# Four rooms for an expert's w2, fetched a whole expert ahead, in an attention, MoE and soft-MoE kernel

## The chip, the cores and the metric

The kernel runs on one core of a Trainium2 chip. The metric is the device time of one launch in microseconds (us). The profile speaks of the core's engines: PE is TensorE's matmul and PEld its weight load (two activities of one engine), DVE is VectorE, ACT ScalarE, POOL GpSimd and SP SyncE, which issues most of the DMAs of this kernel. "SPq" is SyncE's own queue of DMA issues. A DMA issue waits on SyncE until the room that it writes to is free, and all that is issued after it on SyncE waits behind it.

## What is computed

Three layers, one after the other (cut to what matters here):

```python
# 1. attention: batch 4, heads 8, seq 768, head_dim 64; a local window of +-15 keys
#    and the 24 block maxima of k; its output is x, 3072 x 512
x = attn_out.transpose(0, 2, 1, 3).reshape(3072, 512)

# 2. MoE, N 3072 tokens, D 512, E 8 experts, F 1024, cap N // E = 384 tokens each
logits = x @ w_gate
for idx in np.argsort(-logits.flatten()):        # greedy, best pair first
    tok, e = idx // E, idx % E
    if assigned[tok] < 0 and counts[e] < cap:
        assigned[tok] = e; counts[e] += 1
for e in range(E):
    mask = assigned == e
    out[mask] = np.maximum(x[mask] @ w1[e], 0) @ w2[e]

# 3. soft MoE over 32 slots (8 groups of 4)
logits = out @ phi
d = softmax of logits over tokens;  c = softmax of logits over slots
slot_input = d.T @ out                           # 32 x 512
for e in range(8):
    slot_out[e] = np.maximum(slot_input[e] @ w1s[e], 0) @ w2s[e]
result = c @ slot_out
```

The kernel never forms `out`. For expert e it makes h = relu(x w1), the logits as h (w2 phi), the softmax sums from these, and then (d.T h) w2, which has 32 rows instead of 384. The product of w2 and phi is made ahead of the experts.

## The kernel before, in words

The program has four parts: attention; the routing of tokens (the search, many small steps on VectorE with small matmuls called `as`, of which the later ones are spread over the first experts); the experts; and the tail, which is the slot MLPs and the output. Beside the end of attention and the routing, w2 of all experts is loaded, transposed and multiplied by phi (the matmuls of line 1050 with the copies `wt` of line 1065, and `pp` of line 1015). The w2 tiles of experts 1 to 7 for this lie in the pool `pre`, in rooms with the tag "mw", of which there are NPRE1.

**The experts** run in stages r = 0 to 7 of eight steps (fc 0 to 7). A step multiplies the expert's 384 gathered tokens by 128 columns of w1 (`mm1`, line 1260: twelve matmuls into `ph`, since w1 and x are each split into a high and a low part), and transposes an earlier step's result (`turn_h`, line 1281). w1 comes in 256 KB pieces, `raw`, which lie in four rooms; ScalarE casts each into `wh` (line 1225) and GpSimd or VectorE makes `wl` (line 1227), two steps ahead of their use. SyncE issues `raw` four steps ahead of its cast (line 1211).

**The dispatch of expert r-1** is a generator that runs inside stage r. Each step takes it to its next `yield`, so that the two experts' work stands interleaved on TensorE. Near its end, `aT` (the 32 slots' weights times h, summed) is multiplied by w2: eight matmuls of line 1439 into `pS`, in two halves of four. The first half uses quarters 0 and 1 of w2, the second quarters 2 and 3. A quarter is 512 KB. Quarters lie in rooms with the tag "w2", of which there are two, and so the second half is fetched when the first half's matmuls have been issued in the program (`weights2(r, (2, 3))`), and two yields stand between the halves. The first half of the next expert's w2 is fetched after the second (`weights2(r + 1, (0, 1))`). The trace calls these tiles `w`. For the last expert the second half goes into rooms of `raw`.

**The slot MLPs' weights** are 64 pieces of 512 KB, `mw`. Pieces are loaded beside the experts into rooms that are free by then, NPRE of them first (NPRE0 in one pool, NPRE1 in `pre`, the others in a third pool), paced over the 56 steps of stages 0 to 6, then NLATE more once the search is over; then into rooms that the experts no longer need (those of gathered tokens, wh and wl, x, w2, raw). The tail multiplies piece after piece, and a room that has been read takes a further piece.

What sets the order: from the experts on all five engines run in the order of the program text (`manual_schedule`), so the place of a `yield` or of a `weights2` in a generator is the order on each engine's queue. Before that, ScalarE's order is set by the scheduler.

Of the kernel before, what the change touches and what calls it, by code (L numbers as in the profile page):

```python
# [10 lines left out]
F32 = mybir.dt.float32  # L11
# [11 lines left out]
N, DM, E, F = B * S, H * D, 8, 1024  # L23
CAP = N // E
NT = S // 64
NSLOT = 32
NPRE = 28
NHURRY = 2
NSPLIT = 4
NPRE0 = 8  # L30
LAG = 4
WAIT0 = 600
NPRE1 = 19
NLATE = 5
NRAW = 4
NWHL = 3
# [880 lines left out]
def tile_kernel(  # L917
# [13 lines left out]
    nc = tc.nc  # L931
# [180 lines left out]
    ring = ctx.enter_context(tc.tile_pool(name="ring", bufs=2))  # L1112
# [7 lines left out]
    def slot(pool, tag, bufs=None):  # L1120
        return lambda name, dt=F32: [pool.tile([128, 1024], dt, name=name, tag=tag, bufs=bufs)]
# [3 lines left out]
    def halves(pool, tags, bufs):  # L1125
        HALVES.append(
            lambda name: [
                pool.tile([128, 512], F32, name=f"{name}_{i}", tag=tag, bufs=bufs) for i, tag in enumerate(tags)
            ]
        )  # L1130
        return HALVES[-1]
# [30 lines left out]
    with ExitStack() as c2:  # L1162
        wp = c2.enter_context(tc.tile_pool(name="wp", bufs=2))

        XG, EI, ER, W, W2, PR, RAW = {}, {}, {}, {}, {}, {}, []
# [71 lines left out]
        def weights2(r, qs):  # L1237

            for q in qs:
                src = w2[bass.ds(number(r), 1), 256 * q : 256 * q + 256, :].rearrange("o (t p) d->p (o t) d", p=128)  # L1240
                if r + 1 == E and q > 1:

                    ts = [ring.tile([128, DM], F32, name=f"w2_{r}_{q}{i}", tag="raw", bufs=NRAW) for i in range(2)]
                    for i, t in enumerate(ts):
                        nc.sync.dma_start(t, src[:, i])
                    W2[r, q] = ts
                else:
                    t = ring.tile([128, 2, DM], F32, name=f"w2_{r}_{q}", tag="w2", bufs=2)
                    nc.sync.dma_start(t, src)
                    W2[r, q] = [t[:, 0], t[:, 1]]  # L1250

        HT, H, L4 = {}, {}, {}

# [88 lines left out]
        def dispatch(r):  # L1342
# [92 lines left out]
            for cols in (slice(0, 512),):  # L1435
                pS = ps.tile([128, DM], F32, name=f"pS{r}_{cols.start}", tag="b", bufs=2)
                for fc in range(8):
                    g = fc % 4
                    nc.tensor.matmul(  # L1439
                        pS[32 * g : 32 * g + 32, cols],  # L1440
                        aT[:, fc % 2, 32 * (fc // 2) : 32 * (fc // 2) + 32],
                        W2[r, fc // 2][fc % 2][:, cols],
                        start=fc < 4,
                        stop=fc >= 4,
                    )
                    tick(234)
                    if fc == 3 and not last:
                        weights2(r, (2, 3))
                        yield
                        yield  # L1450
                if last:
                    filler(r, 4)
                    for cols in (slice(0, 256), slice(256, 512)):
                        nc.vector.scalar_tensor_tensor(
                            acc[:, cols], acc[:, cols], al, pS[:, cols], ALU.mult, ALU.add
                        )
            if not last:
                weights2(r + 1, (0, 1))
                if r:
                    nc.vector.scalar_tensor_tensor(den, den, al, ds, ALU.mult, ALU.add)  # L1460
                    nc.vector.scalar_tensor_tensor(acc, acc, al, pS, ALU.mult, ALU.add)
                else:
                    nc.vector.tensor_copy(den, ds)
                    nc.vector.tensor_copy(acc, pS)
# [12 lines left out]
        with tc.manual_schedule(engines=engines):  # L1477
            for _ in work:
                if 0 in PLACED:
                    break  # L1480
            while 0 not in PLACED:
                advance()
            gather(0)
            fetch(NRAW - 1)
            while not PP.get("end"):
                next(work)
            split(1)
            weights2(0, (0, 1))
            for dc in range(4):
                transpose_x(0, dc)  # L1490
                if dc:
                    low_x()
                if dc == 0:
                    next(work, None)
            low_x()
        with tc.manual_schedule(engines=engines | {mybir.EngineType.Activation}):
            for r in range(E):
                search_state["stage"] = r
                if r:
                    fetch_p(r)  # L1500
                fill = dispatch(r - 1) if r else iter(())
                next(fill, None)
                for fc in range(8):
                    split(8 * r + fc + NWHL - 1)
                    fetch(8 * r + fc + NWHL - 1 + NRAW)
                    if r == 0 and fc == 1:
                        fetch_p(r)
                    ahead = fc == 7 and r + 1 in XG
                    if ahead:
                        mm1(r, 7, (lambda: None, lambda: transpose_x(r + 1, 0), lambda: transpose_x(r + 1, 1), low_x))  # L1510
                    elif fc == 4:
                        mm1(r, 4, (lambda: None, lambda: logits(r, 0)))
                    elif r == E - 1 and fc in (2, 3):
                        mm1(r, fc, (lambda: None, lambda: next(fill)))
                    else:
                        mm1(r, fc)
                    if r == E - 1 and fc == 7:
                        logits(r, 1, range(3))
                    if fc == 2:
                        next(fill, None)  # L1520
                    while turned < 8 * r + fc - (2 if 8 * r + fc < 8 * E - 3 else 1) + 1:
                        turn_h(*divmod(turned, 8))
                        turned += 1
                    if ahead:
                        low_x()
                    if fc >= 3 and r + 1 in PLACED and r + 1 not in XG:
                        gather(r + 1)
                    if r == E - 1 and fc == 5:
                        weights2(r, (2, 3))
                    if fc != 2:  # L1530
                        next(fill, None)
                    while early and NPRE - len(early) < (NPRE * (8 * r + fc)) // 56:
                        load_pieces(early.pop(0))
                    if search_state["done"] and not late:
                        right.close()
                        late.append(right.enter_context(tc.tile_pool(name="late", bufs=NLATE, side="right")))
                        later += NLATE * [slot(late[0], "mw")]
                    if later and fc % 2:
                        load_pieces(later.pop())
                    if r == E - 1 and fc == 1:  # L1540
                        load_pieces(part(xp.tile([128, 1536], F32, name="xg_mw", tag="xg"), 0))
                    if r == E - 1 and fc >= 6:
                        load_pieces(halves(ring, ("wh", "wl"), NWHL))
                for _ in fill:
                    pass
                if r + 1 < E:
                    while r + 1 not in PLACED:
                        advance()
                    if r + 1 not in XG:
                        gather(r + 1)  # L1550
                        until = search_state["pe"] + 5000
                        while search_state["ready"] < until:
                            advance()
                        search_state["pe"] = max(search_state["pe"], until)
                    for dc in range(4):
                        if dc > 1 or not ahead:
                            transpose_x(r + 1, dc)
                            if len(LOW) > 1:
                                low_x()
                    while LOW:  # L1560
                        low_x()
                    logits(r, 1)
                else:
                    logits(r, 1, (3,))
                    turn_h(r, 7)
                    filler(r, 1)
            x = xp.tile([128, 3072], F32, name="x_mw", tag="x")
            load_pieces(halves(ring, ("wh", "wl"), NWHL), *[part(x, i) for i in range(3)])
            for _ in dispatch(E - 1):
                pass  # L1570
            load_pieces(*2 * [slot(ring, "w2", 2)], *2 * [halves(ring, ("raw", "raw"), NRAW)])


    with ExitStack() as c3:
# [243 lines left out]
```

## Time and profile before

| | |
|---|---|
| median of 3 runs | 572.08 us (571.08 to 574.87) |
| the profiled execution, its own time | 573.06 us |
| its span | 571.4 us, 14592 instructions |
| mean granted TensorE clock | 0.991 of full speed |
| PE busy | 526.3 us (92%) |
| PEld busy | 381.8 us (67%) |
| DVE busy | 343.7 us (60%) |
| ACT busy | 315.8 us (55%) |
| POOL busy | 219.5 us (38%) |
| DMA | 130.61 MB, mean 229 GB/s |

"Busy" is time in which an engine executes something; waits are not in it. The share is over the whole span, and hides that the parts of the program have different limits: the windows below give the same figures for stretches. A wait is written "who <- whom", with total, number of times and longest. A timeline row gives start, duration, engine, line, operation, tile written <- tiles read, partitions and shape, and "x8" for so many instructions joined into one row; brackets hold the idle time ahead of it and what ended it. The trace drops some matmul records, so a row may say x6 where eight were issued. A group such as L1439 is line 1439 of the listing above.

### The profile page before, as it was taken

Reading aid. Unit: us, or ns where it says so; the run is one execution under the profiler, and the core shown is the slowest. Engines: PE = TensorE matmul, PEld = TensorE weight load, DVE = VectorE, ACT = ScalarE, POOL = GpSimd, SP = SyncE. Lnnn points to the kernel's source line nnn. Section 1 sums busy time; section 2 is a strip of 40 time slices with the busy share of each in tenths; the row PEclk is TensorE's granted clock in tenths of the full one; section 3 lists DMA queues with packets and bytes.
Section 4 is the critical chain, followed back from the end, with each engine's and each line's share of the span. In section 5 each row is a group of like instructions: output and inputs, shape, how many; then the busy total and the mean of one; then the engine's idle time right before and its main releaser. Section 6 shows DMA issues by size and latency. Waiting matters only on the chain.

```text
span 571.4 us, 14592 instructions
## 1 busy us (share of the span) xinstructions
PE 526.3 (92%) x5537; PEld 381.8 (67%) x5537; DVE 343.7 (60%) x1111; ACT 315.8 (55%) x670; POOL 219.5 (38%) x264
## 2 busy tenths in 40 slices
PE   4889999999998999998999899999999989999991
PEld 3676877777786766677767576677677858763361
DVE  5688986968854586879788787675232303032152
ACT  2778887868755766435536354544564636321151
POOL 3666554536410003044263552535546472412000
PEclk9999999999999999999999999999999999999996
DMA  9998797996955995355475684765859897679988
GB/s 186 198 193 194 217 170 177 249 220 153 354 168 187 393 341 170 94 172 151 137 241 197 167 269 132 236 202 168 288 166 309 276 312 250 209 270 372 350 260 345
DMA packets 147585, 130.61 MB, mean 229 GB/s; under 512 B 43364, under 2 KB 113636, under 8 KB 147516
## 3 DMA queue, kind: packets, MB, share of 16 engines
q1 hardware_dynamic: 141708, 115.26, 69.3%
q0 software_dynamic: 4368, 13.37, 7.2%
q10 hardware_dynamic: 1440, 1.05, 0.6%
q8 instruction: 44, 0.72, 0.5%
q14 instruction: 25, 0.20, 0.1%
HBM read 113.98 MB, written 14.02 MB: 224 GB/s over the span
## 4 chain that ended last, share of the span: by engine, by line
PE 58%; DVE 20%; DMA 8%; ACT 4%; POOL 3%; SPq 3%; issue 2%; DVEq 0%; POOLq 0%; ACTq 0%
PE ph L1260 17%; PE pwt L1050 4%; DMA w<-in_moe_w_dram 3%; PE pp L1015 3%; PE pt L1281 3%; PE mh L1663 2%; DVE G_r L761 2%; PE pS L1439 2%; PE pS L276 2%; PE l L1301 2%; PE pA L1334 2%; SPq L92 2%; PE po L314 2%; DVE X L288 2%; DVE mn L289 2%
## 5 line engine op out<-in xcount | busy, mean ns | idle before, releaser
L1260 PE MATMUL ph<-x,wh 128*128 128x384 f32 x512 | 145.3, 359 | 0.0
L1227 POOL TENSOR_TENSOR wl<-raw,wh 128x512 fp32r<-128x512 f32 x62 | 82.1, 1325 | 132.3 <-ACT wh L1225 107.6
L1260 PEld LDWEIGHTS ph<-x,wh 128*128 128x128 f32 x512 | 88.5, 189 | 22.2 <-issue 19.4
L1260 PE MATMUL ph<-x,wl 128*128 128x384 f32 x256 | 88.4, 345 | 0.0
L1271 ACT ACTIVATE hT<-ph 128x384 f32<-128x384 f32 x64 | 31.3, 489 | 74.7 <-PE ph L1260 73.8
L293 POOL TENSOR_TENSOR X<-X,mn 128x480 f32<-128x480 f32 x48 | 47.4, 987 | 64.9 <-DVE mn L289 45.0
L1260 PEld LDWEIGHTS ph<-x,wl 128*128 128x128 f32 x256 | 48.1, 188 | 0.0
L1180 POOL DMA_INDIRECT xg<-xd,ids x24 | 23.3, 970 | 61.6 <-PE pwt L1050 52.4
L288 DVE TENSOR_TENSOR X<-pS,nm 128x480 f32<-128x480 f32 x48 | 31.3, 651 | 15.2 <-PE pS L276 14.6
L1225 ACT CAST wh<-raw 128x512 fp32r<-128x512 f32 x64 | 39.9, 623 | 0.0
L1065 ACT COPY wt<-pwt 128x512 f32<-128x512 f32 x60 | 33.1, 591 | 11.0 <-PE pwt L1050 9.5
L222 ACT COPY kT<-pk 64x384 f32<-64x384 f32 x62 | 31.5, 508 | 10.2 <-PE pk L207 9.5
L1050 PE MATMUL pwt<-ident,pw 128*128 128x128 f32 x224 | 33.6, 281 | 1.1 <-ACT wt L1065 0.6
L297 ACT ACTIVATE X<-X 128x480 f32<-128x480 f32 x48 | 29.3, 610 | 9.0 <-POOL X L293 8.2
L1281 PE MATMUL pt<-ident,hT 128*128 128x128 f32 x192 | 33.8, 277 | 0.0
L276 PE MATMUL pS<-kwin,qT 64*64 64x120 f32 x768 | 32.1, 276 | 1.8 <-POOL kwin L244 1.8
L289 DVE TENSOR_REDUCE mn<-X 128x4 f32<-128x480 f32 x48 | 31.3, 653 | 3.7
L1283 ACT COPY h<-pt 128x384 f32<-128x384 f32 x64 | 30.2, 474 | 6.0 <-PE pt L1281 5.8
L1317 POOL DMA_INDIRECT cd<-ce,ids x24 | 25.3, 1053 | 17.4 <-DVE den L1431 13.6
L276 PEld LDWEIGHTS pS<-kwin,qT 64*64 64x64 f32 x768 | 28.1, 138 | 5.0 <-POOL kwin L244 2.4
L314 PEld LDWEIGHTS po<-vw,AT 120*64 120x64 f32 x768 | 24.9, 137 | 8.1 <-issue 3.1
L761 DVE TENSOR_TENSOR G_r<-D_r,as_cn 128x768 bf16<-128x768 bf16 (+1 forms) x41 | 29.3, 713 | 1.2
(299 smaller groups left out, 1053.8 us busy)
## 6 DMA issues: line engine op xcount, KB each, us to landing
mw<-in_moe_w_dram SPq DMA_DIRECT2D x55, 512.0 KB, 6.5
raw<-in_moe_w_dram SPq DMA_DIRECT2D x64, 256.0 KB, 3.4
w<-in_moe_w_dram SPq DMA_DIRECT2D x30, 512.0 KB, 5.8
pw<-in_moe_w_dram SPq DMA_DIRECT2D x28, 512.0 KB, 7.6
vw<-in_v_dram SPq DMA_DIRECT2D x32, 240.0 KB, 6.2
kt<-in_k_dram SPq DMA_DIRECT2D x32, 192.0 KB, 5.1
qt<-in_q_dram SPq DMA_DIRECT2D x32, 192.0 KB, 4.8
xd<-xb POOLq DMA_DIRECT2D x4, 1536.0 KB, 10.4
```

The costliest lines, as they stand in the source:

```text
L276: nc.tensor.matmul(PS[n][i][64 * u : 64 * u + 64, j, :], qT[r, 64 * T : 64 * T + 64], kwin[r, T, :], start=True, stop=True,)
L288: nc.vector.tensor_tensor(X, PS[n][i], nm[:, i // 2], ALU.add)
L289: nc.vector.tensor_reduce(mn, X, AX.X, ALU.min)
L293: nc.gpsimd.tensor_tensor(X, X, MN.pop((n, i))[:, :, None].to_broadcast([128, 4, 120]), ALU.subtract)
L314: nc.tensor.matmul(PO[n][T // 6][64 * (T % 2) : 64 * (T % 2) + 64, T // 2 % 3, hh, :], AT[n, i][0:120, j, 64 * u : 64 * u + 64], vw[0:120, ...
L761: v.tensor_tensor(G, Dg.rearrange("p (q j)->p q j", j=J)[:, :, None, :].to_broadcast([128, 24 // J, n, J]), C["cn", n][:, None].to_broadca ...
L1050: nc.tensor.transpose(pt[:, dc], PW[e, q][t][:, 128 * dc : 128 * dc + 128], ident)
L1065: nc.scalar.copy(wt[:, :, 128 * t : 128 * t + 128], pt)
L1225: nc.scalar.copy(wh, raw)
L1227: (nc.gpsimd if r or u > 1 else nc.vector).tensor_tensor(wl, raw, wh.bitcast(F32), ALU.subtract)
L1260: nc.tensor.matmul(ph, a[:, dc], b[:, dc], start=dc == n == 0, stop=(dc, n) == (3, 2),)
L1281: nc.tensor.transpose(pt[:, c], HT[r, fc][:, 128 * c : 128 * c + 128], ident)
```

## The change

It changes four things.

1. The tag "w2" has four rooms, one for each quarter. The last expert is no exception any more: its quarters 2 and 3 lie in rooms of "w2" as well, not of `raw`.
2. w2 is fetched for the next expert. After the first pS half of expert r, `weights2(r + 1, (0, 1))` is issued, into the rooms just read; after the second half, `weights2(r + 1, (2, 3))`. All four quarters of expert 0 are issued at the start. One `yield` stands between the halves instead of two.
3. NPRE goes from 28 to 26 and NPRE1 from 19 to 17: the two rooms come out of the pool `pre`.
4. In stage 7 the two pairs of `raw` rooms that held the last expert's w2 take two slot MLP pieces (steps 5 and 6), and after the last dispatch the four rooms of w2 take four pieces, where two rooms of w2 and two pairs of raw rooms took them.

Lines from 1249 on stand 7 lower in the changed kernel (1260 is 1253, 1281 is 1274, 1439 is 1432); the DMA of w2 is in line 1242.

```diff
-NPRE = 28
+NPRE = 26
...
-NPRE1 = 19
+NPRE1 = 17
...
 def weights2(r, qs):
             for q in qs:
                 src = w2[bass.ds(number(r), 1), 256 * q : 256 * q + 256, :].rearrange("o (t p) d->p (o t) d", p=128)
-                if r + 1 == E and q > 1:
-
-                    ts = [ring.tile([128, DM], F32, name=f"w2_{r}_{q}{i}", tag="raw", bufs=NRAW) for i in range(2)]
-                    for i, t in enumerate(ts):
-                        nc.sync.dma_start(t, src[:, i])
-                    W2[r, q] = ts
-                else:
-                    t = ring.tile([128, 2, DM], F32, name=f"w2_{r}_{q}", tag="w2", bufs=2)
-                    nc.sync.dma_start(t, src)
-                    W2[r, q] = [t[:, 0], t[:, 1]]
+                t = ring.tile([128, 2, DM], F32, name=f"w2_{r}_{q}", tag="w2", bufs=4)
+                nc.sync.dma_start(t, src)
+                W2[r, q] = [t[:, 0], t[:, 1]]
...
                     if fc == 3 and not last:
-                        weights2(r, (2, 3))
-                        yield
+                        weights2(r + 1, (0, 1))
                         yield
...
             if not last:
-                weights2(r + 1, (0, 1))
+                weights2(r + 1, (2, 3))
...
-            weights2(0, (0, 1))
+            weights2(0, range(4))
...
-                    if r == E - 1 and fc == 5:
-                        weights2(r, (2, 3))
+                    if r == E - 1 and fc in (5, 6):
+                        load_pieces(halves(ring, ("raw", "raw"), NRAW))
...
-            load_pieces(*2 * [slot(ring, "w2", 2)], *2 * [halves(ring, ("raw", "raw"), NRAW)])
+            load_pieces(*4 * [slot(ring, "w2", 4)])
```

TensorE, stage 6, in which the dispatch of expert 5 runs; names carry the expert, then the step or quarter (`w2_5_2` is quarter 2 of expert 5, `ph6_5` step 5 of stage 6). Before:

```order
L1439 MATMUL pS5_0_7520<-w2_5_0_7237,aT5_7479 32x512 x2
L1439 MATMUL pS5_0_7520<-w2_5_1_7239,aT5_7479 32x512 x2
L1260 MATMUL ph6_5_7537<-x_3023,wh6_5_7446 128x384 x2
...
L1281 MATMUL pt6_3_7552<-ident_66,hT6_3_7465 128x128 x3
L1260 MATMUL ph6_6_7565<-x_3023,wh6_6_7488 128x384 x2
...
L1281 MATMUL pt6_4_7581<-ident_66,hT6_4_7512 128x128 x3
L1439 MATMUL pS5_0_7520<-w2_5_2_7525,aT5_7479 32x512 x2
L1439 MATMUL pS5_0_7520<-w2_5_3_7527,aT5_7479 32x512 x2
L1260 MATMUL ph6_7_7606<-x_3023,wh6_7_7531 128x384 x2
```

Now:

```order
L1432 MATMUL pS5_0_7520<-w2_5_0_7155,aT5_7479 32x512 x2
L1432 MATMUL pS5_0_7520<-w2_5_1_7157,aT5_7479 32x512 x2
L1253 MATMUL ph6_5_7537<-x_3023,wh6_5_7446 128x384 x2
...
L1274 MATMUL pt6_3_7552<-ident_66,hT6_3_7465 128x128 x3
L1432 MATMUL pS5_0_7520<-w2_5_2_7203,aT5_7479 32x512 x2
L1432 MATMUL pS5_0_7520<-w2_5_3_7205,aT5_7479 32x512 x2
L1253 MATMUL ph6_6_7577<-x_3023,wh6_6_7488 128x384 x2
```

The second half of pS has moved from two steps behind the first to one.

SyncE at the same place; "ISA" rows are the register reads ahead of a DMA and are left out. Before:

```order
L1211 DMA raw7_2_7492<-in_moe_w1_dram 128x4x128
...
L1249 DMA w2_5_2_7525<-in_moe_w2_dram 128x2x512
...
L1249 DMA w2_5_3_7527<-in_moe_w2_dram 128x2x512
L1156 DMA mw29_7529<-in_moe2_w1_dram 128x2x512
...
L1211 DMA raw7_3_7535<-in_moe_w1_dram 128x4x128
L1156 DMA mw30_7557<-in_moe2_w1_dram 128x2x512
...
L1211 DMA raw7_4_7563<-in_moe_w1_dram 128x4x128
...
L1249 DMA w2_6_0_7590<-in_moe_w2_dram 128x2x512
...
L1249 DMA w2_6_1_7592<-in_moe_w2_dram 128x2x512
```

Now:

```order
L1242 DMA w2_6_0_7525<-in_moe_w2_dram 128x2x512
...
L1242 DMA w2_6_1_7527<-in_moe_w2_dram 128x2x512
L1156 DMA mw27_7529<-in_moe2_w1_dram 128x2x512
...
L1211 DMA raw7_3_7535<-in_moe_w1_dram 128x4x128
...
L1242 DMA w2_6_2_7561<-in_moe_w2_dram 128x2x512
...
L1242 DMA w2_6_3_7563<-in_moe_w2_dram 128x2x512
L1156 DMA mw28_7569<-in_moe2_w1_dram 128x2x512
...
L1211 DMA raw7_4_7575<-in_moe_w1_dram 128x4x128
```

Where the rest of w2 of expert 5 was issued stands the first half of expert 6's, and one step (one `raw`) behind it the second half.

ScalarE ahead of the experts, beside the transposes of w2 for phi (`wt` is such a copy, `pps` one of the products with phi); one piece of the difference:

```order
 L1027 COPY pps4_0_3745<-pp4_0_3586 128x256
+L1225 CAST wh0_0_4085<-raw0_0_3880 128x512
 L1065 COPY wt6_1_3781<-pwt6_10_3750 128x4x128
 L1065 COPY wt6_1_3781<-pwt6_11_3762 128x4x128
-L1225 CAST wh0_0_4085<-raw0_0_3880 128x512
+L1225 CAST wh0_1_4089<-raw0_1_3891 128x512
 L1065 COPY wt6_2_3824<-pwt6_20_3784 128x4x128
```

The first cast of w1 has moved ahead of two copies of w2.

## Rows read from the trace of the kernel before

**Rows 1.** Windows: start:end, length, busy us by engine, PEclk, DMA share, GB/s.
```profile
core 0: us, PE busy (x) PEld busy (x) DVE busy (x) ACT busy (x) POOL busy (x), PEclk, DMA share, GB/s
443.18:474.63 31.45, 29.36 (x199) 22.92 (x199) 6.25 (x16) 15.38 (x36) 16.30 (x17) 1.00 0.89 302
474.63:503.40 28.77, 28.77 (x194) 22.41 (x194) 5.06 (x14) 12.99 (x31) 10.96 (x13) 1.00 0.69 232
511.50:551.30 39.80, 39.01 (x394) 17.13 (x382) 9.35 (x30) 7.74 (x16) 5.55 (x21) 1.00 1.02 340
```

**Rows 2.** Waits of the weight loader and of TensorE, 289 to 475 us.
```profile
PEld pS L1439 <- DMA w<-in_moe_w_dram: 7.2, 6, 2.0
PE pS L1439 <- DMA w<-in_moe_w_dram: 3.2, 4, 1.8
```

**Rows 3.** Timeline of TensorE at the second pS half, stages 1 to 6.
```profile
296.53 1.41 PE L1439 MATMUL pS<-w,aT 128*32 128x512 f32 x8
297.88 0.19 PEld L1260 LDWEIGHTS ph<-x,wh 128*128 128x128 f32 x1 [0.84 <-ACT wh L1225]
...
332.77 1.06 PE L1439 MATMUL pS<-w,aT 128*32 128x512 f32 x8
333.77 0.44 PE L1260 MATMUL ph<-x,wh 128*128 128x384 f32 x1
...
369.57 1.99 PE L1439 MATMUL pS<-w,aT 128*32 128x512 f32 x6
371.49 0.20 PE L804 MATMUL as<-c_r,as_pk 128*128 128x8 f16 x2
...
372.60 0.62 PE L1260 MATMUL ph<-x,wh 128*128 128x384 f32 x2
...
403.00 1.05 PE L1439 MATMUL pS<-w,aT 128*32 128x512 f32 x4
...
405.92 0.62 PE L1260 MATMUL ph<-x,wh 128*128 128x384 f32 x2
...
436.13 1.05 PE L1439 MATMUL pS<-w,aT 128*32 128x512 f32 x4
...
438.38 0.62 PE L1260 MATMUL ph<-x,wh 128*128 128x384 f32 x2
...
467.50 1.05 PE L1439 MATMUL pS<-w,aT 128*32 128x512 f32 x4 [1.79 <-DMA w<-in_moe_w_dram]
...
469.83 0.62 PE L1260 MATMUL ph<-x,wh 128*128 128x384 f32 x2
```

**Rows 4.** Chain of waits that ended last: start, us, what.
```profile
431.59 5.76 DMA w<-in_moe_w_dram
...
462.20 6.60 DMA w<-in_moe_w_dram
...
541.72 9.55 DMA mw<-in_moe_w_dram
```

**Rows 5.** Waits of SyncE's queue of DMA issues.
```profile
SPq L1249 <- PE pS L1439: 18.0, 13, 4.5
```

**Rows 6.** Timeline of VectorE in stage 3.
```profile
371.73 0.17 DVE L815 TENSOR_SCALAR_CACHE_REDUCE ce_r<-as 128x8 bf16<-128x8 f32 x1 [2.65 <-PE as L804]
```

**Rows 7.** The tile `raw`: its loads' time from issue to landing.
```profile
DMA to landing us min/median/max: 2.6/3.4/8.0
```

**Rows 8.** Timeline of ScalarE, TensorE and SyncE around the products with phi.
```profile
200.83 1.07 ACT L1065 COPY wt<-pwt 128x512 f32<-128x512 f32 x2 [0.70 <-PE pwt L1050]
202.05 1.04 PE L1050 MATMUL pwt<-ident,pw 128*128 128x128 f32 x8
203.58 0.44 PE L1050 MATMUL pwt<-ident,pw 128*128 128x128 f32 x2
...
209.04 2.40 SPq L1211 DMA_DIRECT2D raw<-in_moe_w_dram  x4
...
215.72 0.37 ACT L1027 COPY pps<-pp 128x256 f32<-128x256 f32 x1 [0.74 <-PE pp L1015]
```

## The prediction

> **What bounds the kernel now.** I read the times of the engines by stage first, then what TensorE waits for, then the timeline of TensorE at those places, and the chain of waits last. Stage r is the stretch in which expert r's tokens are multiplied by w1 and expert r-1's dispatch runs in the gaps. In stage 7 TensorE is busy for the whole 28.77 us; in stage 6, which holds the same work, it is busy 29.36 of 31.45 us, and the difference is the subject here [rows 1]. The list of waits names it: TensorE and its weight loader stand before the pS matmuls of line 1439 for w2 to land, six times at the loader, 7.2 us in all and 2.0 at most; 3.2 us of it shows at the matmuls too [rows 2]. Of the search, whose steps stand between the matmuls up to about stage 4, only small waits are left. After the experts comes a tail of another kind: from 511.5 to 551.3 us the DMA engines are full (share 1.02, 340 GB/s), and the chain ends this stretch with a 9.55 us load of a slot MLP piece [rows 1, 4].
>
> Why w2 is late: the second half of expert r's w2 may be fetched only when the first half's two rooms have been read, so SyncE issues it behind the first pS half (13 waits of SyncE on pS, 18.0 us) and the second pS half comes two steps later [rows 5]. The loads on the chain took 5.76 and 6.60 us [rows 4]; two steps are about as long, so the second half sometimes comes in time and mostly not.
>
> **The change part by part.**
>
> *The stall goes.* Where w2 is there, the second pS half takes 1.00 us from its start to the next matmul of line 1260 (332.77 to 333.77, stage 2) [rows 3]. Against that:
> - stage 3: 369.57 to 372.60 is 3.03; less 1.00, less 0.20 for a search matmul inside, 1.8
> - stage 4: 403.00 to 405.92 is 2.92; less 1.00, 1.9
> - stage 5: 436.13 to 438.38 is 2.25; less 1.00, 1.25
> - stage 6: 1.79 idle ahead of 467.50, and 467.50 to 469.83 is 2.33; 1.79 + 1.33 is 3.1
> - stage 1: 1.35 instead of 1.00, but the loader behind it waited for the cast of w1 in the same moment, so I take 0 (its ends are 0 and 0.35)
> - stages 2 and 7: nothing [rows 3]
>
> The sum is 1.8 + 1.9 + 1.25 + 3.1 = 8.05 us. After the change all four quarters of an expert's w2 are issued one stage before their use, some 28 us ahead of loads that take 6 to 7, so no such wait can remain. Would something else be late in that moment? In stages 5 and 6 nothing of the search is left beside the products. In stage 3 VectorE itself sat idle 2.65 us until TensorE had done its search matmul behind the stall [rows 6]; it was held up by the stall and moves up with it. So I keep the whole 8.05; its lower end is the sum without stage 3, 6.25, its upper end 8.4 with stage 1.
>
> *The second half moves one step earlier* (two steps behind the first before, one now). TensorE does the same matmuls in another order: 0. The three scatters of an expert move one step earlier on GpSimd, two of them ahead of a subtraction for wl that they formerly stood behind. GpSimd is busy half of stage 6 (16.30 of 31.45 us) [rows 1], and wl is made two steps ahead of its use: 0.
>
> *SyncE's queue.* Per stage it issues the same four w2 loads, at two places that stand one step apart where they stood two steps apart, and each still waits for a pS half. What is queued behind them is raw, the next pieces of w1. Each is issued four steps ahead of its cast, some 14 us (a stage of 28.77 has eight steps), and landed 3.4 us after issue in the median, 8.0 at worst [rows 1, 7]: 0, as long as that cover holds; without it see the third rival.
>
> *Two rooms fewer for early pieces.* By the end of the last dispatch's matmuls 40 of the 64 pieces had been issued before (28 early, 5 late, 1, 6 in the rooms of wh, wl and x), and 40 are now (26, 5, 1, 2 in raw's rooms, 6). The four rooms freed last take four pieces in either. w2 of expert 7 was 2 MB in stage 7 and is; there 1 MB of w2 of expert 6 goes out and 1 MB of pieces comes in. So the tail starts with the same loads outstanding at the same point of the program, is DMA-bound as before, and moves forward as a whole: 0 lost, the 8.05 carries through to the end.
>
> *The pool in which w2 is transposed for phi has 17 rooms, not 19.* A tile takes the room of the 17th before it. The worst case is the third quarter of expert 4: its copy goes into the room of a piece whose transposes end two copies later, at 202.05 + 1.04 = 203.1, where ScalarE started it at 200.83. With 1.07 us for the two copies the first bank is free at about 203.65 where TensorE wanted it at 203.58 [rows 8]: 0.1 us, with 2.3 as the upper end if all of ScalarE's delay came through. The cast of the first raw now stands ahead of two copies on ScalarE: raw was issued at 209.04, so at the worst landing of 8.0 it comes at 217.0, and ScalarE is free for it at 215.72 + 0.37 = 216.1; at worst 0.9 late, and TensorE needs those banks two steps later: 0, upper end 0.9 [rows 7, 8]. The first loads into the pool no longer wait for the stores of the attention's output; nothing on TensorE waited for them, so 0 gained.
>
> **Sum.** 8.05 - 0.1 = 7.95, say 8.0 us. The profiled run took 573.06, which becomes 565.1; it lies 1.0 above the median of the three runs, 572.08, so the median becomes **564.1 us**. With the ends (6.25 less 2.3 and 0.9 is 3.05; 8.4 less nothing) the forecast's own range is 563.7 to 569.0, most of it below 566. Runs of one kernel differ by some us (571.08 to 574.87), which takes it down to 562.
>
> **A rule of the Trainium skill against a row.** DMA in stage 6 was busy 0.89 of 31.45 us, so its work is 28.0 us; the stage is to shrink to 31.45 - 3.1 = 28.35 [rows 1]. By the row it fits with 0.35 us to spare, which is why the first rival has a fifth of the chances. The Trainium skill, page "DMA: Bandwidth & Descriptors", section Bandwidth, has a lone core load at up to 425 GB/s in big transfers. By that figure the stage's 302 GB/s over 31.45 us, 9.5 MB, would need 22.4 us (an estimate), and the first rival would have half its chance; no stretch of this trace ran at it, the fullest (340 GB/s at share 1.02) being well below [rows 1], so I stay with the row.
>
> **The rivals.**
> 1. *DMA becomes the bound of stage 6.* For it: the 0.35 us to spare. Against it: most of those bytes are not needed in that stage (pieces, and w2 of the next expert). If stage 6's 3.1 were given back, 8.0 - 3.1 = 4.9 remain: 567.2. Chance 0.18.
> 2. *The tail gives it back.* It is DMA-bound [rows 1, 4], and if its loads were tied to something that does not move, the time stays 572. Against it: the share is only 0.69 in stage 7, so no work is pent up there, and the rooms of the tail's loads come free by pS of expert 7. Chance 0.08.
> 3. *Raw comes late* (slower). Two pairs of w2 loads now stand one step apart in the queue that brings raw, 2 MB and half a MB of pieces, 7.7 us at 340 GB/s, and raw is behind them. It decides from the point at which raw takes more than its 14 us: at 16 us TensorE would wait 2 us for wh in each of stages 1 to 7, 14 us, less the 8.0: 578. Against it: 8.0 us was the worst landing, in a stage with the DMA at 0.89. Chance 0.07. The Trainium skill, same page, section Queues, rings and completion order, says that each DMA engine takes the descriptors of one queue in order, so raw cannot pass w2. By that rule this rival is what would happen; the worst landing of 8.0 us agrees with it, and shows how small it was so far.
> That the change does not do what it says is excluded by the order: w2 of expert 6 is issued in stage 5's dispatch.
>
> **The numbers.** Forecast 0.67, rivals 0.18, 0.08, 0.07. One per cent, 5.7 us, is about what a measurement of this kernel can tell from no change: 566.4. Below it lie nearly all of the forecast (0.62) and a little of the first rival (0.02): faster 0.64. Within it: the rest of the forecast, the first rival, the second: 0.29. Slower: 0.07. The range is 561.9 to 569.5: the forecast and most of the first rival; it leaves out the second and third, and odd ends.
>
> **What would show it.** Right: no wait of pS on w2; stages 3, 4, 5, 6 shorter by 1.8, 1.9, 1.25, 3.1; the full stretch of the tail as long as before, about 40 us. Wrong: DMA share of 1.0 in stage 6 with waits of line 1260 on wh or wl (first or third rival, by the number of stages); pS of expert 7 early and the last piece's landing not (second); the copies of w2 or their transposes waiting longer between 200 and 220 us (the rooms).

## The result, and the profile after

The changed kernel takes 565.03 us (median of 4 runs, 564.81 to 565.37) where the kernel before took 572.61 (4 runs): ratio 0.987, 95% interval 0.9845 to 0.9894. Forecast were 564.1 us, 561.9 to 569.5, and 0.64 for faster by over 1%. The profiled execution took 565.37 us with a span of 563.6, against 573.06 and 571.4 before; the spans differ by 7.7 us.

The waits of TensorE's matmuls from 240 us on, whole (who <- whom: us in total, times, longest):

```profile
PE as L792 <- DVE G_r L761: 4.5, 8, 1.1
PE as L804 <- DVE c_r L801: 3.7, 5, 1.3
PE px L1195 <- DVE x L1203: 1.2, 3, 0.5
PE po L1708 <- DMA mw<-in_moe_w_dram: 0.8, 1, 0.8
PE as L831 <- DVE B_r L828: 0.7, 2, 0.5
PE pf L1738 <- DVE s L1729: 0.4, 1, 0.4
PE as L701 <- DVE tot_r L688: 0.3, 1, 0.3
```

No wait of pS on w2 is left [rows 2]. The timeline of TensorE at the second pS half in stages 3, 4, 5 and 6 has the form that stage 2 had before, 1.00 us from the start to the next matmul [rows 3]:

```profile
367.70 1.07 PE L1432 MATMUL pS<-w,aT 128*32 128x512 f32 x8
368.69 0.62 PE L1253 MATMUL ph<-x,wh 128*128 128x384 f32 x2
...
400.32 1.07 PE L1432 MATMUL pS<-w,aT 128*32 128x512 f32 x8
401.32 0.62 PE L1253 MATMUL ph<-x,wh 128*128 128x384 f32 x2
...
430.62 1.07 PE L1432 MATMUL pS<-w,aT 128*32 128x512 f32 x8
431.62 0.61 PE L1253 MATMUL ph<-x,wh 128*128 128x384 f32 x2
...
458.89 1.06 PE L1432 MATMUL pS<-w,aT 128*32 128x512 f32 x8
459.88 0.62 PE L1253 MATMUL ph<-x,wh 128*128 128x384 f32 x2
```

The windows of stage 6, of stage 7 up to its last product with w1, and of the full stretch of the tail (columns as in [rows 1]):

```profile
438.79:467.02 28.23, 28.23 (x202) 22.77 (x199) 6.26 (x16) 15.37 (x36) 16.21 (x17) 1.00 0.96 313
467.02:493.29 26.27, 26.27 (x185) 21.34 (x184) 4.76 (x13) 12.02 (x29) 10.86 (x13) 1.00 0.84 285
503.80:543.60 39.80, 39.18 (x394) 16.93 (x382) 9.35 (x30) 7.73 (x16) 5.54 (x21) 1.00 1.01 339
```

TensorE is busy for the whole of stage 6, where it stood still for 2.1 us before; the DMA share has gone from 0.89 to 0.96 there. In stage 7 up to its last product with w1 it has gone from 0.66 to 0.84 (the 0.69 of [rows 1] is of a longer window). The tail's stretch, taken at the same length, has the same share and rate, and the time from the last product with w1 to the end is the same (70.37 and 70.35 us, table below). The chain still ends it with a load of a piece, SyncE waits less often for pS at the fetch of w2 [rows 5], and the worst load of raw is longer [rows 7] (chain; SyncE's waits; the tile raw):

```profile
535.11 8.78 DMA mw<-in_moe_w_dram
```
```profile
SPq L1242 <- PE pS L1432: 14.7, 9, 4.5
```
```profile
DMA to landing us min/median/max: 2.7/3.4/9.8
```

By stage (from the first matmul of `ph` of a stage to that of the next; there are 96 in each, so they can be counted off in the trace; stage 7 ends with its last one):

| stretch | before | after | difference | foreseen |
|---|---|---|---|---|
| up to the experts | 236.08 | 235.62 | -0.46 | +0.1 |
| stage 0 | 30.98 | 30.97 | 0.0 | 0 |
| stage 1 | 36.08 | 36.76 | +0.7 | 0 |
| stage 2 | 36.66 | 37.53 | +0.9 | 0 |
| stage 3 | 37.83 | 36.48 | -1.35 | -1.8 |
| stage 4 | 33.93 | 31.16 | -2.8 | -1.9 |
| stage 5 | 31.55 | 30.27 | -1.3 | -1.25 |
| stage 6 | 31.46 | 28.23 | -3.2 | -3.1 |
| stage 7 | 26.42 | 26.27 | -0.15 | 0 |
| last `ph` to the end | 70.37 | 70.35 | 0.0 | 0 |

Stages 5 and 6 answer to the forecast to 0.1 us. Stages 1 to 4, where most of the search's remaining steps run, sum to -2.6 instead of -3.7, and not one of them is the number that was foreseen.

### The profile page after: what moved, and what is told of

Its sections match the earlier page's. It is cut to its first block, busy times and chain, and to the rows that moved or that the text cites. A ratio compares the mean times of both kernels' runs of the same rounds, so it can differ in the third digit from the quotient of the medians.

```text
span 563.6 us, 14594 instructions
## 1 busy us (share of the span) xinstructions
PE 522.9 (93%) x5537; PEld 381.9 (68%) x5537; DVE 343.5 (61%) x1111; ACT 315.4 (56%) x670; POOL 218.7 (39%) x264
## 3 DMA queue, kind: packets, MB, share of 16 engines
q10 hardware_dynamic: 1440, 1.05, 0.6%
## 4 chain that ended last, share of the span: by engine, by line
PE 61%; DVE 20%; ACT 5%; DMA 5%; issue 3%; POOL 3%; SPq 2%; DVEq 0%; POOLq 0%; ACTq 0%
PE ph L1253 18%; PE pwt L1050 4%; PE pp L1015 3%; PE pt L1274 3%; DVE G_r L761 3%; PE mh L1655 3%; DMA vw<-vw 2%; PE pS L1432 2%; PE pS L276 2%; PE pA L1327 2%; PE l L1294 2%; SPq L92 2%; PE po L314 2%; PE px L1195 2%; DMA mw<-in_moe_w_dram 2%
```

## The experiments

Two questions: is the gain the time between the fetch of w2 and its use, or one of the other edits (the rooms, the place of the second half, the pieces); and what happened in stages 1 to 4. "Before" in the ratios is the kernel before, run beside each group.

**Cover of one step less.** The kernel before with one yield between the halves:

```diff
                         weights2(r, (2, 3))
                         yield
-                        yield
```

> The kernel before with one yield between the pS halves instead of two; rooms, fetch places and pieces as before. Theory of distance (the gain comes from the time between the fetch of w2 and its use): one step of some 3.4 us is taken from the cover, so the wait at the second half grows by 3.4 us in stages 3 to 6 (13.6), and appears in stage 1 (3.4), stage 2 (3.3) and stage 7 (2.6): some 22 us slower, 588 to 597 us. Rival, that the second half's earlier place on TensorE is itself worth something: 565 to 572 us. Rival, that fewer loads beside w2 are what helped: no change, 572 us.

598.21 us, ratio 1.0475 (1.0423 to 1.0527). The theory's direction holds, and of its size the sum, not the stages: +25.8 us is just above the range, and it comes unevenly, 6.8 us in stage 1 (3.4 expected), 0.7 in stage 3 (3.4) and 5.0 in stage 7 (2.6). The second half's earlier place does not make up for the lost cover. The wait of the matmuls on w2 has grown from 3.2 us [rows 2] to this:

```profile
PE pS L1439 <- DMA w<-in_moe_w_dram: 17.3, 12, 4.4
```

TensorE's granted clock adds to it. In stage 1 TensorE stood still for 2.00 us up to 294.57 (first row; then windows, columns as in [rows 1]):

```profile
294.57 1.46 PE L1439 MATMUL pS<-w,aT 128*32 128x512 f32 x4 [2.00 <-DMA w<-in_moe_w_dram]
```
```profile
294.00:295.00 1.00, 0.43 (x2) 0.14 (x4) 1.00 (x1) 0.00 (x0) 1.00 (x2) 1.00 1.08 389
...
297.00:298.00 1.00, 1.00 (x4) 0.00 (x0) 0.00 (x0) 0.00 (x0) 0.00 (x0) 0.50 1.00 297
...
301.00:302.00 1.00, 1.00 (x6) 0.69 (x6) 0.01 (x1) 0.00 (x0) 0.00 (x0) 0.55 1.07 373
302.00:303.00 1.00, 1.00 (x8) 0.96 (x9) 0.64 (x4) 0.16 (x1) 0.00 (x0) 1.00 0.97 290
```

PEclk is 0.50 (1.2 of 2.4 GHz) from about 295 to 302, so behind this wait TensorE works at the lower level for some 7 us. The trace has five such stretches between 295 and 517 us, 23.9 us together; the profile of the kernel before, whose longest wait on w2 is 1.8 us, has none there.

**Cover of one step more.** The kernel before with a third yield, still with two rooms and 28 pieces:

```diff
                         weights2(r, (2, 3))
+                        yield
                         yield
                         yield
```

> The kernel before with three yields between the pS halves; still two rooms for w2, 28 and 19 pieces. Theory of distance: one step more of cover, 3.4 us, is longer than every wait that before had (3.1 at most), so all waits of pS on w2 go without any further room: 572.6 less 8 is 564.6 us (563.5 to 566.5). Rival, that the rooms or the fewer pieces did it: 572 us. If the tail needs the later w2 or scatters: 566 to 570 us.

566.05 us, ratio 0.990 (0.9877 to 0.9923), and no wait of pS on w2 in the list. So two rooms are enough for most of the gain, if the fetch stands three steps ahead of the use. One yield 598, two 572, three 566: with the rooms unchanged, the time follows the distance.

**The rooms without the fetch ahead.** The changed kernel, but an expert's quarters 2 and 3 are fetched where they were before:

```diff
-                        weights2(r + 1, (0, 1))
+                        weights2(r, (2, 3))
+                        yield
                         yield
...
-                weights2(r + 1, (2, 3))
+                weights2(r + 1, (0, 1))
+                if r + 2 == E:
+                    weights2(r + 1, (2, 3))
...
-            weights2(0, range(4))
+            weights2(0, (0, 1))
```

> The changed kernel with its four rooms and 26 pieces, but quarters 2 and 3 of an expert are fetched where before fetched them (after its first pS half), and two yields stand between the halves. Theory of distance: SyncE reaches the fetch just after a load of w1, at the time of the first half, whether or not the room is free (in stage 6 of before w1 was issued at 460.96 and w2 at 461.59 us), so the waits stay: 571 to 573 us. Rival, that rooms alone give it: 565 us.

**The fetch ahead with the old place of the halves.** The changed kernel with a second yield:

```diff
                         weights2(r + 1, (0, 1))
                         yield
+                        yield
```

> The changed kernel with two yields between the pS halves as before; rooms, fetch of the next expert and pieces as changed. Theory of distance: w2 has landed a stage ahead either way, so 565 us, within 1 us; the steps of the search return nearly to their places of before, so that stages 1 and 2, which grew by 0.7 and 0.9 us in the changed kernel, return to 36.1 and 36.7 us, and stages 3 and 4 to their old length less 1.8 and 1.9. Rival, that the second half's earlier place is a part of the gain: 567 to 569 us.

The rooms alone: 571.72 us, ratio 1.0001 (0.9976 to 1.0026). With the fetch ahead: 564.57, ratio 0.9881 (0.9857 to 0.9906). These two differ in the fetch alone, same yields, rooms and pieces. The matmuls of the first wait for w2 four times, 3.5 us in all (3.2 in the kernel before); those of the second do not. TensorE in stage 6, first the rooms alone:

```profile
457.82 1.06 PE L1432 MATMUL pS<-w,aT 128*32 128x512 f32 x8
...
465.75 1.05 PE L1432 MATMUL pS<-w,aT 128*32 128x512 f32 x4 [1.82 <-DMA w<-in_moe_w_dram]
467.06 1.05 PE L1432 MATMUL pS<-w,aT 128*32 128x512 f32 x4 [0.26 <-DMA w<-in_moe_w_dram]
468.05 0.62 PE L1253 MATMUL ph<-x,wh 128*128 128x384 f32 x2
```

then with the fetch ahead:

```profile
454.76 1.06 PE L1432 MATMUL pS<-w,aT 128*32 128x512 f32 x8
...
460.80 1.06 PE L1432 MATMUL pS<-w,aT 128*32 128x512 f32 x8
461.80 0.62 PE L1253 MATMUL ph<-x,wh 128*128 128x384 f32 x2
```

A free room brings nothing while the fetch stands where it stood; from the start of the first half to the matmul of line 1253 behind the second half it is 10.2 us in the one and 7.0 in the other. Stages 1 to 4 of the second run take 35.7, 37.0, 36.9 and 32.0 us: 1, 2 and 4 came within 0.4 us of what was expected, but stage 3 is 36.9 instead of 36.0, with no wait on w2. Its timeline shows why:

```profile
368.82 1.06 PE L1432 MATMUL pS<-w,aT 128*32 128x512 f32 x6
369.81 0.20 PE L804 MATMUL as<-c_r,as_pk 128*128 128x8 f16 x2
369.95 1.05 PE L1432 MATMUL pS<-w,aT 128*32 128x512 f32 x2
370.92 0.62 PE L1253 MATMUL ph<-x,wh 128*128 128x384 f32 x2
```

Nothing waits here, and yet the half takes 2.10 us instead of 1.00 with a search matmul of 0.20 inside. The view of the tile w in the changed kernel, from 400 to 500 us, gives the duration of one record of pS (minimum, median, maximum in ns):

```profile
L1432 PE MATMUL pS<-w,aT x56: 592/605/617, 400.3 to 481.8; 128*32 128x512 f32 x56
```

Eight such records fit into 1.06 us, so they run side by side (each matmul has 32 weight columns, and the four of a half write to different quarters of the rows of `pS`). When a matmul with 128 weight columns comes in between, the two records behind it take as long as all eight. In the changed kernel the search step falls into the second half of stage 2 instead:

```profile
330.81 1.06 PE L1432 MATMUL pS<-w,aT 128*32 128x512 f32 x6
331.80 0.18 PE L817 MATMUL as<-cd_r,as_o 128*128 128x1 bf16 x1
331.91 1.04 PE L1432 MATMUL pS<-w,aT 128*32 128x512 f32 x2
332.88 0.61 PE L1253 MATMUL ph<-x,wh 128*128 128x384 f32 x2
```

**The price of a matmul inside a half, by itself.** The changed kernel with a matmul that nobody uses (128 weight columns, 8 columns moved), eight times in stages 4 to 7, `g == 1` inside the half or `g == 3` behind it:

```diff
+                    if r in (3, 4, 5, 6) and g == 1:
+                        pw = ps.tile([128, 128], F32, name=f"probe{r}_{fc}", tag="c", bufs=2)
+                        nc.tensor.matmul(pw[:, 0:8], ident, ident[:, 0:8], start=True, stop=True)
                     tick(234)
```

> The changed kernel with a matmul more that nobody uses (128 weight columns, 8 columns moved) in each pS half of the dispatches of experts 3 to 6, put between the second and the third of its four matmuls: eight of them, where nearly nothing of the search is left. Theory, that such a matmul breaks up matmuls which run side by side on quarters of TensorE: each half takes some 2.0 to 2.1 instead of 1.00 us, as pS of stage 2 did with a search matmul inside, so 8 times 1.0 to 1.1 is 8 to 9 us: 573 to 574 us. Rival, that it costs what its own row says, 0.1 to 0.2 us: 566 to 567 us.

> The same eight matmuls, each put behind its half instead of inside. Theory: 8 times 0.1 to 0.3 us, 565.8 to 567.5 us, and every half at 1.0 us. Rival, that any matmul of another shape there costs 1 us, wherever it stands: 573 us as the run with the matmul inside.

Inside 575.85 us, ratio 1.0033 (1.0008 to 1.0059); behind 567.44, ratio 0.9883 (0.9837 to 0.993). They stand 8.4 us apart, 1.05 for each. Behind, the time lies in the range that was expected; inside, it is 1.85 us above it. Inside (the first half in stage 6):

```profile
459.70 1.05 PE L1432 MATMUL pS<-w,aT 128*32 128x512 f32 x4
460.69 0.39 PE L1441 MATMUL probe<-ident 128*128 128x8 f32 x2
461.00 1.05 PE L1432 MATMUL pS<-w,aT 128*32 128x512 f32 x4
461.99 0.62 PE L1253 MATMUL ph<-x,wh 128*128 128x384 f32 x2
```

behind:

```profile
458.14 1.06 PE L1432 MATMUL pS<-w,aT 128*32 128x512 f32 x8
459.14 0.39 PE L1441 MATMUL probe<-ident 128*128 128x8 f32 x2
459.38 0.59 PE L1253 MATMUL ph<-x,wh 128*128 128x384 f32 x2
```

From the start of the half to the next matmul of line 1253 it is 2.28 us inside (461.99 less 459.70) and 1.24 behind (459.38 less 458.14), against 1.00 without the extra matmul. So the same matmul adds 0.24 us behind the half and 1.28 inside, in all eight halves; what the theory left out, and why its range was passed, is that the matmul's own time comes on top of the 1.0 for the broken half. Whether a matmul of 32 weight columns would break the half up as well was not tried.

**Groups kept whole.** The changed kernel with the search's chances behind a group:

```diff
-                    tick(234)
+                    if g == 3:
+                        for _ in range(4):
+                            tick(234)
...
-                    tick(127)
+            for _ in range(12):
+                tick(127)
...
-                tick(181)
+            for g in gs:
+                tick(181)
```

> The changed kernel, but no step of the search is put between the matmuls of one group on TensorE (the four of a pS half, the twelve of pA, the four of a half of the logits l); the same chances for a search step come behind each group. In the changed kernel's trace a group with a search matmul inside takes longer: pS of stage 2 2.07 instead of 1.00 us, pA of stages 1 to 3 2.09, 2.93 and 3.18 instead of 1.43, four halves of l 1.67 to 1.83 instead of 0.78: 8.9 us over in all. Theory, that a full-width matmul put inside breaks up matmuls which run side by side on quarters of TensorE: some 1.5 us of the 8.9 is the search's own, the rest goes: 565.0 less 5 to 7, 558 to 560 us. Rival, that VectorE's search steps are the limit of stages 1 to 3 and the groups only wait for them: 564 to 566 us, with waits of TensorE on G_r and c_r (4.5 and 3.7 us now) that grow by the same.

> The changed kernel with two yields between the halves and with the groups kept whole. Theory, that the two edits don't bear on each other: 564.6 less the 2.3 us that whole groups gave is 562.3 us (561.3 to 563.5), and the waits of TensorE on the search's G_r, c_r and B_r are longer than with groups broken up (11.2 us). Rival, that two yields put the search's steps elsewhere and the gain is lost: 564.6 us.

562.71 us, ratio 0.9822 (0.9795 to 0.9849), and with two yields 562.14, 0.9796 (0.975 to 0.9841). All of their runs (558.92 to 564.54) lie below the changed kernel's lowest, 564.81; the two are not to be told from each other. All groups are whole in the trace (pA 1.44, l 0.78, pS 1.00 us; one pS of stage 1 takes 1.2 for another wait), but 2.3 us came instead of 5 to 7: the rival held for a part. TensorE's waits on the search, in the first of them:

```profile
PE as L792 <- DVE G_r L761: 5.9, 9, 1.3
PE as L804 <- DVE c_r L801: 3.7, 5, 1.3
PE as L831 <- DVE B_r L828: 1.4, 3, 0.5
...
PE as L804 <- DVE pr_r L638: 0.6, 2, 0.4
```

That is 11.6 us where the changed kernel has 8.9 with the same operations: TensorE waits 2.7 us more for VectorE, which is what is missing from the lower end of the 5 to 7.

**Are the pieces worth what was said?** The kernel before with two rooms fewer for early pieces, and the changed kernel without the two pieces in rooms of raw:

```diff
-NPRE = 28
+NPRE = 26
...
-NPRE1 = 19
+NPRE1 = 17
```

> The kernel before with 26 and 17 rooms for early pieces instead of 28 and 19, nothing else: two pieces of 512 KB are loaded later, in the tail. Theory of the prediction (the tail is bound by its loads): 1.05 MB at 340 GB/s is 3.1 us, so 575.5 us (574.5 to 576.5), and the stretch from the last pS to the end grows from 59.0 to 62; the start of the experts stays at 236 us, since two rooms fewer cost the products with phi nothing. Rival, that fewer loads beside the experts shorten the waits on w2: 569 to 571 us. Rival, that the tail is TensorE's: no change, 572.4 us.

```diff
-                    if r == E - 1 and fc in (5, 6):
-                        load_pieces(halves(ring, ("raw", "raw"), NRAW))
...
-            load_pieces(*4 * [slot(ring, "w2", 4)])
+            load_pieces(*4 * [slot(ring, "w2", 4)], *2 * [halves(ring, ("raw", "raw"), NRAW)])
```

> The changed kernel without the two pieces that it loads into rooms of raw in stage 7; those rooms are filled after the last dispatch, behind w2's four. Theory, that the tail is bound by its loads: it grows as it did with two early pieces fewer in the kernel before (59.0 to 61.0 us), so 567 us (566 to 568.5). Rival, that the loads have time enough in the tail: 565 us.

577.53 us, ratio 1.0081 (1.005 to 1.0112), that is 4.4 us slower than before's 573.18 beside it, where 3.1 were expected; and 567.94, ratio 0.9919 (0.9894 to 0.9945), 2.9 above the changed kernel. In both profiles the stretch from the last pS to the end is longer by some 2.1 us (61.0 and 61.1 instead of 59.0; 62 was expected of the first), and the wait of `po` on pieces in the tail is the place, first the kernel before with fewer rooms, then the changed one:

```profile
PE po L1716 <- DMA mw<-in_moe_w_dram: 2.4, 4, 0.9
```
```profile
PE po L1706 <- DMA mw<-in_moe_w_dram: 2.0, 3, 0.9
```

So the tail is bound by its loads. A piece costs 1.05 us there by the profiles and 1.45 by the median of the second run; 512 KB at the tail's 340 GB/s would be 1.5. In the first of these runs the second half of pS still waited for w2, 3.5 us in all: fewer loads beside the experts do not shorten that wait. The 4.4 us of the medians are not wholly found in the profile, whose own execution took 574.98 us.

**Is DMA the next bound of stage 6?** The changed kernel with two or six copies of 512 KB in stage 6 that nobody waits for, from device memory to device memory, on SyncE's queue (shown for six):

```diff
+                    if r == E - 2 and fc in range(6):
+                        src = m2w1[0:2, 0:128, 0:512].rearrange("g p f->p g f")
+                        nc.sync.dma_start(spare.pop().rearrange("p (g f)->p g f", g=2), src)
```

> The changed kernel with two more loads of 512 KB on SyncE's queue in stage 6 (steps 2 and 4), from and to device memory, that nobody waits for. DMA is busy 0.96 of stage 6's 28.23 us in the changed kernel, so 1.1 us is free, and at 340 GB/s 1.05 MB takes 3.1. Theory, that most bytes of stage 6 are not needed in it: stage 6 stays at 28.2 us and stage 7 (share 0.84) takes the rest over: 565 us. Rival, that DMA is the bound of stage 6: 2 us more in stage 6, 567 us, with waits of TensorE or ScalarE on raw or w.

> The changed kernel with six such loads (steps 0 to 5 of stage 6), 3.1 MB, 9.2 us at 340 GB/s. Theory: stage 6 at most 1 us longer; 9.2 less the 1.1 free in stage 6 and the 4.2 in stage 7 is 3.9 us, by which the slot MLPs' pieces come later and the tail grows: 568 to 570 us. Rival, that DMA is the bound of stage 6: 8 us more in stage 6, 573 us or more. If raw loads behind the extra ones take over 14 us: waits of ScalarE on raw in stage 6.

564.93 us with two (one execution). With six 565.81, ratio 0.9871 (0.9838 to 0.9905), the changed kernel's own ratio, and the tail from the last pS on is 59.0 us long, as without them: the theory's 568 to 570 did not come. Stages 6 and 7 in the profile with six:

```profile
438.64:466.87 28.23, 28.23 (x202) 22.77 (x199) 6.26 (x16) 15.35 (x36) 16.20 (x17) 1.00 1.06 370
466.87:493.25 26.38, 26.38 (x185) 21.25 (x184) 3.77 (x13) 12.14 (x29) 10.87 (x13) 1.00 1.00 339
```

Stage 6 is as long as without the extra copies, and stage 7 by 0.1 us longer. The rate went from 313 to 370 GB/s in stage 6 and from 285 to 339 in stage 7, which is 1.6 and 1.4 MB more, together nearly all of the 3.1: the copies were not put off, they found room. The share of 0.96 had promised 1.1 us of free time in stage 6, some 0.4 MB at 340 GB/s; so neither that share nor 340 GB/s was the limit there. ScalarE waited once for raw in the experts, 1.8 us in stage 7, and TensorE did not.

## Why the prediction was right, and where a term was not

*The mechanism* was right, and the runs show it: with the distance between fetch and use the waits come and go (598, 572, 566 us); rooms without distance bring nothing (ratio 1.0001), and at the same rooms, yields and pieces the fetch ahead is worth 1.2%.

*The stall, 8.05 us.* Stages 1 to 7 are shorter by 7.2 us together. That is near the sum, but two of the terms were wrong. Stage 3 was put at 1.8, with 0.20 taken off for the search matmul inside the half. That matmul costs 1.10 there, since it breaks the half up: 3.03 less 2.10 leaves 0.9 for the wait on w2, and the run with two yields, which has the same broken half and no wait, shortens stage 3 by 0.9. The step that failed is "less 0.20 for a search matmul": the row's own duration was taken for its price. With 0.9 the waits on w2 are 0.9 + 1.9 + 1.25 + 3.1, some 7.2 us in all.

*"TensorE does the same matmuls in another order: 0"* fell for the same reason. The moved yield shifts the search's steps. They no longer fall into pS of stage 3 and a half of l in stage 4 (1.68 instead of 0.78 us there before), which gave 2.0 us, but into pS of stage 2 (1.07 us over) and into halves of l in stages 1 and 2 (0.9 each). In stage 4, 1.9 of w2 and 0.9 of l make the measured 2.8. Stage 2 grew by 0.9, while its groups grew by 2.4 (pA of stage 2 takes 0.4 more as well); in the two traces TensorE's waits for the search's steps on VectorE in this stage went from 3.2 us (G_r 2.0, B_r 0.6, c_r 0.6) to 1.5 (G_r 1.3, B_r 0.2), which is most of the rest. In stage 3 the half of pS is 2.0 shorter and the stage 1.35; 0.5 of the difference is a new wait of line 1195 for the tile x, which VectorE makes (the row of px above). Keeping the groups whole gives 2.3 us.

That the total came so near is therefore in part luck. Beside w2, the stages changed by +0.7, +0.9, -0.4 and -0.9 in 1 to 4, which nearly cancels and which nothing in the forecast foresaw; and 0.46 of the 7.7 us between the spans lies ahead of the experts (next term). "In stages 5 and 6 nothing of the search is left" was not quite so either: a half of l in stage 5 is broken up by a search step (1.68 us), before and after alike, so that it drops out of the difference.

*The rooms for phi* cost nothing: the 0.46 us that the experts start earlier are already there at 197 us (the same copy of ScalarE starts at 197.26 and at 196.79), and between profiles whose programs do not differ up to there the start moves as much (before 236.08, one yield 235.61); so it is a spread between executions and no term. The kernel before with 17 rooms in that pool started its experts at 235.90. Neither upper end, 2.3 or 0.9, reached TensorE: ScalarE stood 0.6 us for the first raw at 216.22, and no matmul waited longer for it.

*SyncE's queue.* The worst load of raw took 9.8 us, against a cover of 14: hidden, as forecast. With six copies more in that queue ScalarE waited 1.8 us for raw, and no stage grew by more than 0.1 us. The Trainium skill, page "DMA: Bandwidth & Descriptors", section Queues, rings and completion order, has a DMA engine take one queue's descriptors in order, though a later one may finish its write first, so that the prediction's "raw cannot pass w2" says more than the page. The longer landings agree with it, and in the changed kernel no load of raw whose landing the trace tells came in ahead of a load of w2 or a piece issued before it; its price here was nothing.

*The pieces.* Two in raw's rooms make up for two early ones, and the tail is as long as before. Loaded late instead they cost 2.9 us (2.1 of it seen in the tail): the cover named in the forecast was needed.

*The rivals.* The first (DMA as the bound of stage 6, 0.18) is refuted beyond its own margin: 0.35 us were thought free, and the stage took 1.6 MB more without growing. The margin came from taking a share of 0.89 for 28.0 us of work, and that does not hold as a limit: the share rose to 1.06 and the rate to 370 GB/s in the same time. Nor is 340 GB/s the most that the DMA reaches: one of the 40 slices of the profile's page shows 393 GB/s before and 397 after. The prediction's other reason, that bytes which are not needed in the stage may come late, was not put to the test, since they did not come late. A share near 1 alone tells nothing: in the tail it is 1.01, and there two pieces more do cost time. The second (the tail gives it back) did not happen: the tail moved forward as a whole. The third (raw late) did not come, and with 3.1 MB more in the queue it cost TensorE nothing.

## What to carry to other kernels

Read a wait for a load as a distance: the time from issue to landing less the time from issue to use. Another buffer helps only if the issue moves with it, and moving the use (one more yield) is worth nearly as much without any memory. A high DMA share does not show that DMA bounds a stage: add copies that nobody waits for and look whether the stage grows. And the price of an instruction inside a group is what the group takes with it, less what it takes without it, not the instruction's own row.

## Seen of the hardware, and not expected

Four matmuls of 32 weight columns each that write to different quarters of the rows run side by side: eight records of about 0.6 us in 1.06. One matmul with 128 weight columns between them, 0.2 to 0.4 us by its row, adds 1.1 to 1.3 us, and the one of 0.39 us behind them adds 0.24. And behind a wait TensorE can run slower for a time: after the standstill up to 294.57 us in the run with one yield the granted clock was 0.50 for some 7 us, and two matmuls of `ph` in a row took 0.84 us at 301.05 instead of 0.51 at 302.11. The wait alone does not settle it: in stage 6 of the kernel before, 1.8 us of standstill on w2 were followed by no such stretch, and the run with the matmuls behind the halves has one from 365.7 us, behind a wait of 1.5 us for the search.
